# Decode attention: y accumulated as 4 rows of 128 columns and stored in 256-byte pieces

## The chip, the cores and the metric

The kernel runs on one core of a Trainium2 chip. The profile shows five engines that work side by side: TensorE (PE, busy for 479.8 us of the span of 680.7 us in the kernel before, with its weight loads as PEld, 264.9 us), VectorE (DVE, 377.8 us), ScalarE (ACT, 42.5 us), GpSimd (POOL, 2.4 us) and SyncE (SP), which here issues loads and stores. In the kernel they wait for one another by semaphores. The page counts 16 DMA engines; in the kernel before they read 285.21 MB from HBM, nearly all of it into a ring in the on-chip memory SBUF. The kernel has PE's sums in tensors of PSUM. The metric is the time of one execution on the device in microseconds (us). Each profile is one execution; its span is 1.7 to 2.0 us shorter than the reported time of the same run.

## The reference, cut to what matters

Two independent attention problems A and B of one query token, with the same shapes; the outputs are concatenated.

```python
# x (1,1,512)  k,v (1,32,8192,128)  wq (512,4096)  wo (4096,512), all bf16
q = (x @ wq) as 32 heads of 128
scores = einsum("bhqd,bhkd->bhqk", q, k) * 128 ** -0.5
o = softmax(scores) @ v                # 32 heads of 128 numbers
y = o.reshape(1, 1, 4096) @ wo         # 512 numbers for each problem
out = concatenate([y_A, y_B], axis=-1) # 1024 bf16, 2 KB
```

K and V of both problems are 268 MB, and each number is used once. The output is 2 KB.

## The kernel before

The heads are done in pairs: `j` runs over 32 pairs, 16 of A and 16 of B. Each K or V of a pair is one load of 4 MB into a ring of five slots; all loads are issued by SyncE. For a pair, DVE multiplies K by q, PE adds up partial columns with an identity matrix ("fold"), DVE, PE and ACT do the softmax, and PE multiplies V by the probabilities ("PV": 128 matmuls with a moving operand of 2 columns).

The part that the change touches is y = o times W_o. Each head needs four matmuls, each of which loads a 128x128 block of W_o as weights and streams one column of o. The 512 outputs lie in PSUM as 128 partitions of 4 columns, so that the store writes 128 pieces of 8 bytes:

```python
def plan_y(a, h0, n, pm):            # heads h0..h0+n of problem a
    ...
    wo = ring[...].rearrange("p (h m b) -> p h m b", h=H, b=NB)      # NB = 4
    for i in range(n):
        for b in range(NB):
            m = e.matmul(y_ps[:, b:b + 1], wo[:, h0 + i, :, b],
                         src[:, a, h0 + i:h0 + i + 1], ...)
    if lastblk:
        ...
        ve = INC('DVE', c_ye, lambda e: e.tensor_copy(y_sb[:, a, :], y_ps[:, 0:NB]))
        W('SP', c_ye, ve)            # the store waits in SyncE's program order
        ... e.dma_start(out[0, 0, a * NOUT:(a + 1) * NOUT].rearrange("(p b) -> p b", b=NB),
                        y_sb[:, a, :])                               # issued by SP
```

The y of A is computed some 400 us into the run, while loads of B stream. The y of B ends the run. Its heads come in groups: 16, 8 and 4 heads while the last pair's softmax is under way, then two heads after PV(30) and two after PV(31):

```python
j = NPR - 1                          # 31, the last pair
plan_R(j, 1); plan_w_ready(j - 2)
plan_y(LA, *ys.pop(0))               # 16 heads, 64 matmuls
plan_m1(j); plan_tr(j)               # maxima of the pair; transposed on PE
plan_y(LA, *ys.pop(0))               # 8 heads, 32 matmuls
plan_m2(j); plan_bc(j); plan_exp(j); plan_sum(j); plan_ri(j)
for b in ys: plan_y(LA, *b)          # 4 heads, 16 matmuls
for i in range(2):
    plan_PV(j - 1 + i); plan_o(j - 1 + i)
    plan_y(LA, *direct_l[i])         # 2 heads, 8 matmuls
```

## Time and profile before

| | before |
|---|---|
| time, median of 3 runs (lowest, highest) | 683.43 us (682.38, 684.32) |
| span of the profile | 680.7 us |
| last K landed / last V landed | 643.7 / 674.9 us |
| last store: issued / landed | 676.54 / 680.30 us |

Landing times that no line below shows are read from the landing records of the trace: the moments at which a transfer's semaphore is counted up.

From the page of the kernel before, the DMA rows of the 40 time slices: the busy share in tenths, then the rate.

```profile
span 680.7 us, 12357 instructions
...
DMA  9999999999999999999999999999999999999993
GB/s 370 431 430 431 431 433 429 429 430 430 427 435 433 428 430 432 430 426 430 431 430 429 431 430 430 428 405 432 429 432 432 428 426 430 430 430 433 422 415 131
```

The DMA engines are busy from end to end at about 430 GB/s, so the run is bound by loads; one slice, the 27th, shows 405. The next view gives three stretches of 12 us: length, then busy time of PE, PEld, DVE, ACT and POOL (with the number of instructions), granted PE clock (the share of its full speed that PE was allowed), DMA share and, last, GB/s.

```profile
423.00:435.00 12.00, 11.47 (x159) 6.84 (x160) 8.70 (x13) 0.04 (x1) 0.00 (x0) 0.86 1.00 426
...
439.00:451.00 12.00, 6.43 (x144) 4.63 (x141) 3.73 (x5) 0.00 (x0) 0.00 (x0) 0.84 1.00 392
451.00:463.00 12.00, 8.93 (x26) 3.56 (x27) 7.84 (x12) 1.14 (x5) 0.00 (x0) 0.64 1.01 437
```

In the middle stretch the DMA engines are as busy as ever but move 392 GB/s. In exactly this stretch the 128 small writes of A's y are carried out (their packets start between 439.55 and 447.23 us): they wait in the queue behind loads, and their landing records lie between 440.2 and 447.8 us, the last 37.4 us after the issue. The view of the tile `y_sb` gives both stores, A's and B's:

```profile
L552 SPq DMA_DIRECT2D out_dram<-y_sb x2: 344/388/431, 410.4 to 676.5; - x2
...
DMA to landing us min/median/max: 3.8/20.6/37.4
```

The tail is read from the chain of waits, the work that ended last, in order of time (start, length, what):

```profile
605.27 38.42 DMA ring<-in_B_k_cache_dram
...
648.41 5.31 PE fold L374 x16
...
656.47 3.63 PE fold L374 x16
...
660.18 2.14 PE yps L537 x64
...
662.52 1.03 PE yps L537 x32
...
665.93 0.52 PE yps L537 x16
666.46 3.43 PE otps L459 x128
...
670.13 0.43 PE yps L537 x8
...
670.88 1.51 issue
672.39 3.25 PE otps L459 x116
...
676.35 0.16 DVE y_sb L546
```

From the landing of the last K at 643.7 us on, PE, DVE and ACT work in turn: two folds, the y groups between the steps of the softmax, PV(30) from 666.46, PV(31) with a pause of 1.51 us after its first 12 matmuls, the cast, and then the store. "issue" marks time in which the engine waited for nothing that the profile shows.

### The profile page before, as it was taken

To read this page: it belongs to the slowest core of one execution; us is meant where nothing else is said; L and a number is where in the kernel's file an instruction comes from. 1 tells how busy PE (TensorE), PEld (TensorE's weight loads), DVE (VectorE), ACT (ScalarE), POOL (GpSimd) and SP (SyncE) were. 2 spreads that over 40 slices of the span, in tenths; PEclk is the share of its full clock that TensorE was granted. 3 is DMA by queue.
4 is the path that set the end of the run, shared out by engine and by line. 5 is a ranking of instruction groups with operands and counts; after the bars stand their busy time and mean duration, and the time that the engine had idled before them with its cause. 6 is when DMAs were issued, how large, how long until landed. Compare 5 with 4: busy or idle time off the path is not lost.

```text
span 680.7 us, 12357 instructions
## 1 busy us (share of the span) xinstructions
PE 479.8 (70%) x5660; PEld 264.9 (39%) x5660; DVE 377.8 (56%) x513; ACT 42.5 (6%) x169; POOL 2.4 (0%) x16
## 2 busy tenths in 40 slices
PE   0487877767688767856777576857768768667775
PEld 0133533434343434433433352534434234334445
DVE  4158556655555665555556526656555557463650
ACT  0110000000000000000000000000000001000000
POOL 1000000000000000000000000000000000000000
PEclk9998867877876867789867786967887668678885
DMA  9999999999999999999999999999999999999993
GB/s 370 431 430 431 431 433 429 429 430 430 427 435 433 428 430 432 430 426 430 431 430 429 431 430 430 428 405 432 429 432 432 428 426 430 430 430 433 422 415 131
DMA packets 11684, 286.01 MB, mean 420 GB/s; under 512 B 1776, under 2 KB 2288, under 8 KB 2672
## 3 DMA queue, kind: packets, MB, share of 16 engines
q1 hardware_dynamic: 11344, 285.22, 97.9%
q8 instruction: 44, 0.72, 0.4%
q14 instruction: 8, 0.07, 0.0%
q10 hardware_dynamic: 288, 0.00, 0.0%
HBM read 285.21 MB, written 0.00 MB: 419 GB/s over the span
## 4 chain that ended last, share of the span: by engine, by line
DMA 53%; PE 30%; DVE 12%; issue 3%; ACT 1%; ACTq 0%; DVEq 0%
DMA ring<-in_B_k_cache_dram 27%; DMA ring<-in_A_k_cache_dram 22%; PE fold L374 19%; DVE ring L361 11%; PE otps L459 7%; DMA xT<-in_B_x_dram 3%; PE qwps L333 2%; PE yps L537 1%; ACT qbc L340 1%; DVE m L410 1%; ACT p L429 0%; PE stps L436 0%; PE stps L405 0%; DVE wt L504 0%; PE stps L415 0%
## 5 line engine op out<-in xcount | busy, mean ns | idle before, releaser
L374 PE MATMUL fold<-ring,ident 128*128 128x512 bf16 x1024 | 320.5, 484 | 109.7 <-DVE ring L361 109.2
L361 DVE TENSOR_TENSOR ring<-ring,qbc 128x2048 bf16<-128x2048 bf16 x256 | 300.9, 1216 | 148.5 <-DMA ring<-in_A_k_cache_dram 84.9
L374 PEld LDWEIGHTS fold<-ring,ident 128*128 128x128 bf16 x1024 | 117.3, 120 | 287.8 <-issue 117.5
L459 PEld LDWEIGHTS otps<-p,ring 128*128 128x128 bf16 x4096 | 108.3, 97 | 8.7 <-issue 1.6
L459 PE MATMUL otps<-p,ring 128*128 128x2 bf16 x4096 | 108.3, 163 | 1.5 <-issue 1.5
L387 DVE TENSOR_REDUCE s_sb<-fold 128x64 f32<-128x512 f32 x64 | 43.1, 674 | 10.7 <-PE fold L374 10.3
L410 DVE TENSOR_REDUCE m<-stps 2x1 f32<-2x128 f32 x32 | 8.9, 279 | 69.8 <-PE stps L405 69.8
L436 PE MATMUL stps<-rowsum,ones_f 128*128 128x2 f32 x64 | 13.6, 282 | 41.5 <-ACT p L429 41.5
L421 ACT COPY nb<-stps 128x1 f32<-128x1 f32 x32 | 5.1, 159 | 580.3 <-PE stps L415 580.3
L333 PE MATMUL qwps<-ring,xsel 128*128 128x512 bf16 x64 | 16.7, 408 | 29.2 <-DVE xsel L226 24.3
L429 ACT ACTIVATE p<-s_sb,nb 64x128 bf16<-64x128 f32 x64 | 27.9, 436 | 2.1 <-ACT nb L421 0.3
L436 PEld LDWEIGHTS stps<-rowsum,ones_f 128*128 128x128 f32 x64 | 10.8, 211 | 44.2 <-ACT p L429 44.2
L333 PEld LDWEIGHTS qwps<-ring,xsel 128*128 128x128 bf16 x64 | 6.0, 103 | 39.4 <-issue 27.2
L415 PE MATMUL stps<-m,sel 2*128 2x1 f32 x64 | 12.3, 259 | 11.5 <-DVE m L410 11.5
L415 PEld LDWEIGHTS stps<-m,sel 2*128 2x128 f32 x64 | 9.6, 186 | 24.0 <-DVE m L410 24.0
L397 DVE TENSOR_REDUCE m<-s_sb 64x1 f32<-64x128 f32 x64 | 17.7, 277 | 1.0
L504 DVE TENSOR_TENSOR wt<-qwps,hmask 128x512 f32<-128x512 f32 (+3 forms) x5 | 2.2, 440 | 24.6 <-PE qwps L497 24.5
L429 ACT ACTIVATION_READ_ACCUMULATOR p<-s_sb,nb 64x1 f32 x64 | 11.7, 182 | 0.0
L475 DVE TENSOR_TENSOR ot<-otps,rinv 128x2 bf16<-128x2 f32 x32 | 4.9, 154 | 11.8 <-PE otps L459 11.8
L537 PE MATMUL yps<-w_bf,ring 128*128 128x1 bf16 x240 | 8.7, 172 | 1.9 <-issue 1.9
L537 PEld LDWEIGHTS yps<-w_bf,ring 128*128 128x128 bf16 x240 | 8.6, 118 | 1.9 <-issue 1.9
L405 PE MATMUL stps<-ident_f,m 128*2 128x128 f32 x32 | 8.8, 275 | 0.0
(30 smaller groups left out, 34.4 us busy)
## 6 DMA issues: line engine op xcount, KB each, us to landing
ring<-in_A_k_cache_dram SPq DMA_DIRECT2D x16, 4096.0 KB, 37.1
ring<-in_A_v_cache_dram SPq DMA_DIRECT2D x16, 4096.0 KB, 31.0
ring<-in_B_k_cache_dram SPq DMA_DIRECT2D x16, 4096.0 KB, 37.8
ring<-in_B_v_cache_dram SPq DMA_DIRECT2D x15, 4096.0 KB, 31.9
ring<-in_A_wq_dram SPq DMA_DIRECT2D x1, 4096.0 KB, 12.5
ring<-in_B_wq_dram SPq DMA_DIRECT2D x1, 4096.0 KB, 21.9
ring<-in_A_wo_dram SPq DMA_DIRECT2D x1, 4096.0 KB, 36.5
ring<-in_B_wo_dram SPq DMA_DIRECT2D x1, 2048.0 KB, 20.2
```

Of the source, the lines that this page charges most:

```text
L333: m = e.matmul(qw_ps[:, :].rearrange("p (j d) -> p j d", d=Dh), xsel[:, a, c, par, :], wq[:, c, 4 * g:4 * g + 4, par, :], start=(i == 0), ...
L361: m_val[(j, i)] = INC('DVE', c_m, lambda e: e.tensor_tensor(t, t, qbc[:, a, jj:jj + 1, :].broadcast_to([P, CH, Dh]), ALU.mult))
L374: m = e.matmul(fold_ps[h][:, :].rearrange("p (t e) -> p t e", e=FE), ident[:], t[:, h * HT:(h + 1) * HT, c * FE:(c + 1) * FE], start=(c == ...
L387: r_val[(j, h)] = INC('DVE', c_r, lambda e: e.tensor_reduce(s_sb[:, j % 2, h * HT:(h + 1) * HT], fold_ps[h][:, :].rearrange("p (t e) -> p ...
L397: m1_val[j] = INC('DVE', c_m1, lambda e, h=h, q0=q0, q1=q1: e.tensor_reduce(m1[q0:q1, j % 2, h:h + 1], s_sb[q0:q1, j % 2, :], AX.X, ALU.max))
L405: tr_val[j] = INC('PE', c_tr, lambda e: e.transpose(st_ps[j % 2][0:2, 0:P], m1[:, j % 2, :], ident_f[:]))
L410: m2_val[j] = INC('DVE', c_m2, lambda e: e.tensor_reduce(m2[0:2, j % 2:j % 2 + 1], st_ps[j % 2][0:2, 0:P], AX.X, ALU.max))
L415: bc_val[j] = INC('PE', c_bc, lambda e: e.matmul(st_ps[j % 2][:, P:P + 1], sel2[:], m2[0:2, j % 2:j % 2 + 1], start=True, stop=True))
L429: e_val[j] = INC('ACT', c_e, lambda e, h=h, q0=q0, q1=q1: e.activation(p2[q0:q1, j % 2, :, h], s_sb[q0:q1, j % 2, :], AF.Exp, bias=nb[q0:q ...
L436: s_val[j] = INC('PE', c_s, lambda e: e.matmul(st_ps[j % 2][:, P + 2:P + 4], ones_f[:], rowsum[:, j % 2, :], start=True, stop=True))
L459: m = e.matmul(ot_ps[j % 2][:, 0:2], t[:, i, :], p2[:, j % 2, i, :], start=(i == 0), stop=(i == TP - 1))
L537: m = e.matmul(y_ps[:, b:b + 1], wo[:, h0 + i, :, b], src[:, a, h0 + i:h0 + i + 1], start=(first and i == 0 and b == 0), stop=(lastblk and ...
```

## The change

The intent: write the output in longer pieces. The roles in the y matmul are swapped. W_o streams, 128 columns at a time, and the weights are a narrow matrix of 4 columns, one of which holds o. For each head, `sq` is a 4x4 square with o on its diagonal, so that matmul `b` uses row `b` of the square and adds its 128 numbers to row `b` of PSUM. y is then 4 partitions of 128 columns, and a store is four pieces of 256 bytes. The y of A is stored from ACT's queue instead of SyncE's.

```diff
-        y_sb = ec(nc.sbuf_tensor("y_sb", [P, NA, NB], BF16))
+        y_sb = ec(nc.sbuf_tensor("y_sb", [NB, NA, P], BF16))
+        sq = ec(nc.sbuf_tensor("sq", [P, NA, H, NB * NB], BF16))
...
     # plan_o, last two pairs: o straight onto the diagonal
+                o_val[j] = INC('DVE', c_o, lambda e: e.tensor_tensor(
+                    sq[:, a, 2 * jj:2 * jj + 2, 0:NB * NB:NB + 1], ...))
...
     # plan_w, other heads: one more DVE copy onto the diagonal
+                w_val[(a, h0)] = INC('DVE', c_w, lambda e, i0=i0: e.tensor_copy(
+                    sq[:, a, h0 + i0:h0 + i0 + ni, 0:NB * NB:NB + 1], ...))
...
-                    "p (h m b) -> p h m b", h=H, b=NB)
+                    "p (h b m) -> p h b m", h=H, b=NB)
...
-                        m = e.matmul(y_ps[:, b:b + 1], wo[:, h0 + i, :, b], src[:, a, h0 + i:h0 + i + 1],
+                        m = e.matmul(y_ps[0:NB, 0:P], sq[:, a, h0 + i, b * NB:(b + 1) * NB],
+                                     wo[:, h0 + i, b, :],
...
-                W('SP', c_ye, ve)
+                q = 'SP' if a == LA else 'ACT'
+                W(q, c_ye, ve)
...
-                            out[0, 0, a * NOUT:(a + 1) * NOUT].rearrange("(p b) -> p b", b=NB),
+                    out[0, 0, a * NOUT:(a + 1) * NOUT].rearrange("(b m) -> b m", b=NB),
```

## The prediction

> **What bounds the kernel.** DMA. In the span of 680.7 us the page's DMA row reads 9 nearly everywhere, at about 430 GB/s; SyncE's waits for free slots (484.5 us on the PE fold) hide behind queued loads. The tail differs: the last K lands at 643.7 us, then (chain of waits, timeline) fold to 660.1, y matmuls of early heads (64, 32, 16) between softmax steps, PV(30) 666.3 to 669.9, 8 y matmuls, PV(31) to 675.6 with a 1.51 us stall at 670.9, 8 y matmuls, cast at 676.35, store issued at 676.54, landed 3.8 us later. The last V piece lands at 674.9 in the landing records: DMA and PE end nearly together.
>
> **What the change removes.**
> 1. The first y store (128 pieces of 8 B) sits in the SP queue among the loads and lands 37.4 us after issue. Windows show 392 GB/s over 439 to 451 us, 429 to 431 around it: about 0.09 of 12 us, so 1 us of every DMA engine, critical. [...] Worth 0.6 to 1.0 us.
> 2. The last store: its landing records spread over 678.0 to 680.3 us, as 16 engines finish 8 small writes each. With 4 pieces I expect 1.6 to 2.2 us from issue to landing, not 3.8. Worth 1.6 to 2.2 us, all critical.
>
> **What it adds.**
> 1. Each y matmul loads 4 columns and streams 128; before, 128 loaded and 1 streamed. Before: 64 in 2.28 us, 36 ns each. After: the fold takes 227 ns per 512 columns at full clock and 427 at half (timeline), so I estimate 57 to 65 ns each warm and 107 cold. [...] The granted clock is 0.50 after 665 us, so the late ones are cold. On the tail chain the 64 delay the transpose of the maxima by about 1.4 us, the 32 the broadcast by 0.6, the 16 add 0.3 to 1.1, and the two groups of 8 add 0.2 to 0.5 each: 2.5 to 4 us, partly returned because the 1.51 us stall, [...], should shrink when PE comes later.
> 2. First problem: 128 y matmuls at 403 to 410 us take 7 to 14 us instead of 6.4. Off the path: several loads of 9.7 us each are queued.
> 3. The cast reads 128 elements per partition, not 4: about 0.28 us (the maximum over 2x128 takes 0.279), not 0.16. Diagonal copies and memset are hidden.
>
> **Sum.** −0.8 (first store) −1.9 (last store) +1.9 (y in the tail, net of the stall's return, 0.5 to 3.5) +0.1 = about −1 us: 682.4 us, range 680.2 to 684.6. Faster by over 2%: 0.01; within 2%: 0.98; slower: 0.01.
>
> **What would show it.** GB/s near 440 to 460 us level at about 430; last V landing about 1 us earlier; last store landing under 2.3 us after issue; y matmuls at 57 to 65 ns in the first group, about 107 in the last; PV(30) starting 1 to 3 us later; a shorter stall.
>
> **What would make it wrong.** Load-plus-stream pairs well over 65 ns warm; HBM writes landing no sooner in 256 B pieces; the stall not shrinking; the first store's cost not being on the slowest engine's path.

The sum came to −0.8 − 1.9 + 1.9 + 0.1 = −0.7 us, put as about −1 us. The first term rests on the dip to 392 GB/s alone. The pace of 57 and 107 ns stands as an estimate from the fold's 227 and 427 ns for 512 columns, a quarter of each.

## The result, and the profile after

| | before | after |
|---|---|---|
| first comparison: median (lowest, highest) | 683.3 us (682.38, 684.32), 4 runs | 684.04 us (683.82, 684.24), 4 runs |
| ratio of after to before, 95% interval | | 1.001 (0.9993 to 1.0028) |
| second comparison (after_2 below): median | 682.87 us, 11 runs | 682.38 us (681.78, 684.26), 6 runs |
| ratio, 95% interval | | 0.9996 (0.9979 to 1.0012) |

A ratio is the mean time of one kernel's runs over that of the other's of the same rounds, so it is not quite the ratio of the medians. The kernel was neither faster nor slower. What matters is where the gains went.

The first store. The same view of stretches, after:

```profile
439.00:451.00 12.00, 9.19 (x148) 5.83 (x148) 6.98 (x9) 1.14 (x5) 0.00 (x0) 0.86 1.02 437
451.00:463.00 12.00, 9.48 (x37) 4.14 (x38) 7.30 (x12) 1.14 (x5) 0.00 (x0) 0.86 1.00 430
```

The dip is gone. The last K lands at 642.76 us instead of 643.69, the last V at 674.00 instead of 674.88.

The last store. SyncE's wait at the end of the program for the output to land (total, times, longest), first before, then after:

```profile
SPq L99 <- DMA out_dram<-y_sb: 3.4, 1, 3.4
```

```profile
SPq L100 <- DMA out_dram<-y_sb: 0.8, 1, 0.8
```

From the issue at 680.17 us to the last landing record at 681.36 us it took 1.19 us. Before, it took 3.8.

The tail, from the chain of waits of the changed kernel:

```profile
606.79 35.97 DMA ring<-in_B_k_cache_dram
...
647.47 6.26 PE fold L378 x16
...
656.48 5.18 PE fold L378 x16
...
661.74 3.67 PE yps L550 x64
...
665.60 1.88 PE yps L550 x32
...
669.46 0.98 PE yps L550 x16
670.44 3.33 PE otps L463 x128
...
674.03 1.01 PE yps L550 x8
675.04 3.52 PE otps L463 x128
...
678.82 1.03 PE yps L550 x8
...
679.87 0.28 DVE y_sb L561
```

Three things differ. The y groups take 3.67, 1.88 and 0.98 us instead of 2.14, 1.03 and 0.52, and the last two 1.0 us each instead of 0.43. The pause inside PV(31) is gone. And the two folds, which the change does not touch, take 6.26 and 5.18 us instead of 5.31 and 3.63.

The second profile of the unaltered changed kernel, after_2, shows that the folds are a matter of the run, not of the kernel:

```profile
647.41 5.09 PE fold L378 x16
...
655.25 3.63 PE fold L378 x16
...
667.66 3.31 PE otps L463 x128
...
672.65 0.63 issue
673.28 3.25 PE otps L463 x116
```

With folds alike, the two kernels can be compared stage by stage. Each row is a difference of times in the chain of waits; the last two use the landing records and the span.

| stage | before | after_2 | difference | after, first profile: difference from before |
|---|---|---|---|---|
| start to last K landed | 643.69 | 642.70 | −0.99 | −0.93 |
| to the end of the last fold | 16.41 | 16.18 | −0.23 | +2.49 |
| to the start of PV(30) | 6.36 | 8.78 | +2.42 | +2.42 |
| to the end of PV(31) | 9.18 | 8.86 | −0.32 | −1.06 |
| to the end of the cast | 0.87 | 1.59 | +0.72 | +0.72 |
| to the landing of the last store | 3.79 | 1.21 | −2.58 | −2.58 |
| to the end of the span | 0.40 | 0.73 | +0.33 | +0.34 |
| sum | 680.70 | 680.05 | −0.65 | +1.40 |

The two stores won 0.99 + 2.58 = 3.57 us. The tail gave back 2.42 − 0.32 + 0.72 = 2.82 us, for y matmuls that are slower and a larger cast, and 0.1 us elsewhere. What is left is 0.65 us, which the 2 us that one run of this kernel differs from the next hides.

### The profile page after: what moved, and what is told of

It reads as the page before. It is cut to its first block, busy times and chain, and to the rows that moved or that the text cites. A ratio compares the mean times of both kernels' runs of the same rounds, so it can differ in the third digit from the quotient of the medians.

```text
span 682.1 us, 12363 instructions
## 1 busy us (share of the span) xinstructions
PE 481.2 (71%) x5660; PEld 270.6 (40%) x5660; DVE 379.1 (56%) x519; ACT 42.5 (6%) x169; POOL 2.5 (0%) x16
## 2 busy tenths in 40 slices
DMA packets 11411, 286.00 MB, mean 419 GB/s; under 512 B 1504, under 2 KB 2016, under 8 KB 2400
## 4 chain that ended last, share of the span: by engine, by line
DMA 53%; PE 32%; DVE 12%; issue 2%; ACT 1%; ACTq 0%; DVEq 0%
DMA ring<-in_B_k_cache_dram 27%; DMA ring<-in_A_k_cache_dram 22%; PE fold L378 19%; DVE ring L365 11%; PE otps L463 7%; DMA xT<-in_B_x_dram 3%; PE yps L550 3%; PE qwps L337 2%; ACT qbc L344 1%; DVE m L414 1%; PE stps L409 0%; DVE wt L514 0%; DVE w_bf L523 0%; ACT p L433 0%; DVE xsel L230 0%
## 5 line engine op out<-in xcount | busy, mean ns | idle before, releaser
L378 PE MATMUL fold<-ring,ident 128*128 128x512 bf16 x1024 | 312.9, 475 | 115.0 <-DVE ring L365 114.9
L378 PEld LDWEIGHTS fold<-ring,ident 128*128 128x128 bf16 x1024 | 115.4, 118 | 287.6 <-DVE ring L365 120.4
L550 PE MATMUL yps<-ring,sq 128*4 128x128 bf16 x256 | 18.9, 244 | 0.5 <-DVE sq L480 0.5
L550 PEld LDWEIGHTS yps<-ring,sq 128*4 128x4 bf16 x256 | 17.5, 96 | 0.9 <-DVE sq L480 0.7
```

Of the source, the lines that this page charges most:

```text
L378: m = e.matmul(fold_ps[h][:, :].rearrange("p (t e) -> p t e", e=FE), ident[:], t[:, h * HT:(h + 1) * HT, c * FE:(c + 1) * FE], start=(c == ...
L550: m = e.matmul(y_ps[0:NB, 0:P], sq[:, a, h0 + i, b * NB:(b + 1) * NB], wo[:, h0 + i, b, :], start=(first and i == 0 and b == 0), stop=(las ...
```

## The experiments

Twelve kernels ran, in three sets; each set has its own runs of the kernel before. "Ratio" is always to those. All gave the reference's output except the two marked.

| run | median us | before, same set | ratio (95% interval) |
|---|---|---|---|
| t_first | 682.15 | 682.75 | 0.999 (0.9976 to 1.0004) |
| t_last | 681.24 | 682.75 | 0.9973 (0.9959 to 0.9987) |
| t_both | 681.02 | 682.75 | 0.9971 (0.9957 to 0.9985) |
| after_order | 682.42 | 682.75 | 0.9985 (0.997 to 1.0) |
| first_act8 | 683.66 | 683.88 | 1.0003 (0.9978 to 1.0027) |
| first_sp256 | 683.84 | 683.88 | 1.0002 (0.998 to 1.0024) |
| last8 (wrong) | 685.64 | 683.88 | 1.0029 (1.0005 to 1.0052) |
| shift64 | 683.09 | 683.88 | 1.0003 (0.9971 to 1.0035) |
| after_2 | 682.38 | 682.87 | 0.9996 (0.9979 to 1.0012) |
| after_warm | 680.42 | 682.87 | 0.9962 (0.9948 to 0.9976) |
| t_order | 680.05 | 682.87 | 0.9958 (0.9944 to 0.9972) |
| last32 (wrong) | 682.27 | 682.87 | 0.9994 (0.9976 to 1.0012) |

None differs from the kernel before by 2%; the interval leaves out 1 for t_last, t_both, after_warm and t_order (shorter) and for last8 (longer).

### The two stores without the new matmuls: t_first, t_last, t_both

These keep the one-column y matmuls and turn the finished y on PE, one small transpose for a problem, for A only, for B only, and for both.

```diff
+ y_f = ec(nc.sbuf_tensor("y_f", [P, NA, NB], F32))
+ y_t = ec(nc.sbuf_tensor("y_t", [NB, NA, P], BF16))
-    "p (h m b) -> p h m b", h=H, b=NB)
+    "p (h b m) -> p h b m" if a in TR else "p (h m b) -> p h m b", h=H, b=NB)
+ if a in TR:                                   # TR = (0,), (1,) or (0, 1)
+     tensor_copy(y_f[:, a, :], y_ps[:, 0:NB])                       # DVE
+     transpose(y_ps[0:NB, P:2 * P], y_f[:, a, :], ident_f[:])       # PE
+     tensor_copy(y_t[:, a, :], y_ps[0:NB, P:2 * P])                 # DVE
+     store y_t[:, a, :] as "(b m) -> b m", from ACT for A, from SP for B
```

> The kernel before; only y of the first problem is transposed on TensorE (after a copy to SBUF) and stored in four 256-byte pieces from the ACT queue; y matmuls keep one moving column; the last store stays 128 pieces of 8 bytes. Theory (the first store's 8-byte pieces cost every DMA engine about 0.9 us and the run is DMA bound): no dip to 392 GB/s in 439 to 451 us, last K and last V land 0.8 to 1.0 us earlier than in the kernel before (643.7 and 674.9), the time is 0.5 to 1.0 us shorter, last store still about 3.8 us from issue to landing. Rival (the tail hides what the loads win): V lands earlier, but the time stays within 0.3 us of before.

Measured: the window 439 to 451 us shows 433 GB/s, no dip. The last V landed at 674.20 us. The mean time is 682.23 us against 682.87, 0.6 us less, but the interval of the ratio includes 1. So the loads do end earlier; that the time follows is likely and not shown by this run alone.

> The kernel before; only y of the second problem is transposed on TensorE and stored in four 256-byte pieces; its W_o weights are read contiguously. Theory: last store lands 1.2 us after issue instead of 3.8 (as after the change), the added copy, transpose and copy cost about 0.8 us, so the time is 1.5 to 2.2 us shorter; the last V still lands at about 674.9. Rival (the short landing in the changed kernel comes from the DMA queues being idle longer before it, not from the pieces): landing stays near 3 us and the time is within 0.5 us or longer.

Measured: issued to landed about 1.2 us, the last V at 674.86 us, and 1.8 us less in the mean (681.04 against 682.87), as the theory had it. The rival, that the DMA queues had only been idle for longer, is settled by last8 below: its small pieces were issued 5.3 us after the last V had landed, later than the 3.7 us here, and still took 3.6 us. So the gain of the last store is in the pieces.

> Both of the above. Theory (the two gains add): 2.3 to 3.0 us shorter than before, about 680.7 us, and the same below the changed kernel 684.0 by 3 us or more, since the stores are the same and only the y matmul form differs. Rival (the form of the y matmuls costs nothing in the tail and the changed kernel is slow for the clock phase alone): within 1 us of the changed kernel.

Measured: 2.1 us less than before in the mean (680.73 against 682.87), a little under what was expected; the first store adds only 0.3 us to t_last, within the scatter. Against the changed kernel the ratio is 0.9971 / 0.9996 (after_2, another set) = 0.9975, about 1.7 us less, where 3 us was expected from the unlucky first measurement of 684.04. The timeline of t_both shows what binds its tail, with PE now early enough:

```profile
672.67 0.58 PE L463 MATMUL otps<-p,ring 128*128 128x2 bf16 x16 [0.23 <-DMA ring<-in_B_v_cache_dram]
...
673.91 0.58 PE L463 MATMUL otps<-p,ring 128*128 128x2 bf16 x16 [0.66 <-DMA ring<-in_B_v_cache_dram]
...
675.38 0.38 PE L553 MATMUL yps<-ident_f,y_f 128*4 128x128 f32 x1 [0.26 <-DVE y_f L551]
...
675.79 0.28 DVE L556 CAST y_t<-yps 4x128 bf16<-4x128 f32 x1 [0.47 <-PE yps L553]
```

PV(31) waits for each part of the last V: the tail is bound by the loads, as it should be. The transpose with its copies adds about 0.74 us: from the end of the last y matmul to the end of the cast it takes 0.93 us here (675.14 to 676.07), and 0.19 in the kernel before (676.32 to 676.51).

### Piece size or queue: first_act8, first_sp256

The change altered both for A's store. Each run undoes one of them.

```diff
 first_act8, from the kernel before
-                W('SP', c_ye, ve)
+                q = 'SP' if a == NA - 1 else 'ACT'
+                W(q, c_ye, ve)             # and the store is issued from q
 first_sp256, from the changed kernel
-                q = 'SP' if a == LA else 'ACT'
+                q = 'SP'
```

> The kernel before with the first y store issued from the ACT queue, still 128 pieces of 8 bytes. Theory (the piece size costs, not the queue): the DMA engines still lose 0.7 to 1.0 us each, now soon after 410 us (the dip moves there), the store lands within some 10 us of issue, and last K and V land as before. Rival (the place in the SP queue costs): no dip, last K and V 0.9 us earlier.

> The changed kernel with the first y store back on the SP queue, still four 256-byte pieces. Theory: no dip anywhere, the store lands some 30 to 37 us after issue, last V lands as in the changed kernel (674.0 in its profile) and the time is within 0.4 us of the changed kernel. Rival: the dip of 0.9 us is back and the time 0.9 us longer.

Windows of first_act8:

```profile
411.00:423.00 12.00, 8.56 (x25) 3.50 (x26) 8.52 (x13) 1.14 (x5) 0.00 (x0) 0.64 1.00 410
...
439.00:451.00 12.00, 9.27 (x150) 5.92 (x148) 6.55 (x8) 1.14 (x5) 0.00 (x0) 0.86 1.00 431
```

Windows of first_sp256:

```profile
439.00:451.00 12.00, 9.25 (x148) 5.84 (x148) 6.82 (x8) 1.14 (x5) 0.00 (x0) 0.86 1.01 434
```

With 8-byte pieces on ACT's queue the dip moved to the stretch after 411 us; it landed 15.3 us after issue, later than the 10 us expected, and the last V landed at 674.78 us, as before. With 256-byte pieces on SyncE's queue there is no dip, though the store again waited among the loads (issued at 411.8, landed at 443.2 us), and the last V landed at 674.13. The piece size costs, and the queue does not. How deep the dip is varies: in 439 to 451 us the three profiles with an 8-byte first store from SyncE show 392 (before), 403 (shift64) and 414 GB/s (t_last), the ten with 256-byte pieces 425 to 437. Over all profiles: the last V landed at 674.88, 674.86, 674.78 and 674.22 us with an 8-byte first store (mean 674.69) and between 673.68 and 674.20 us in the ten with 256-byte pieces (mean 673.93), 0.76 us earlier. The 674.22 of shift64 lies outside its group, and why is open.

### What a store of small pieces costs: last8, last32

From the changed kernel, the last store is cut into pieces of 8 or 32 bytes that are interleaved by partition. The second half of the output is therefore permuted.

```diff
-    out[0, 0, a * NOUT:(a + 1) * NOUT].rearrange("(b m) -> b m", b=NB), y_sb[:, a, :]
+    dst.rearrange("(g b e) -> b g e", b=NB, e=4),        # last32: e=16
+    y_sb[:, a, :].rearrange("b (g e) -> b g e", e=4)     # last store only
```

> The changed kernel with the last store cut on purpose into 128 pieces of 8 bytes from its 4 partitions, to places interleaved by partition, so the second half of the output is permuted (a wrong result on purpose). Theory (each small HBM write takes its time on its engine, 8 per engine took 1.5 to 3.8 us from issue): 32 pieces on each of 4 engines land 5 to 10 us after issue and the time grows by 4 to 9 us. Rival (the number of engines or partitions sets the landing): 1.2 us as in the changed kernel.

> As last8 (landing 3.6 us after issue with 128 pieces of 8 bytes on 4 engines), but 32 pieces of 32 bytes, again permuted on purpose. Theory (a store to HBM takes a time for each piece, whatever engine it comes from: 2.4 us more for 124 more pieces): about 1.7 to 1.9 us from issue to landing. Rival (pieces below some size are slow however few): 3 us or more. Second rival (pieces do not matter at 32 bytes): 1.2 us.

Measured: last8 was issued at 679.36 us and landed at 682.99, 3.6 us. That is as long as in the four profiles that store the same 128 pieces from 128 partitions (3.8 us before, 3.5 to 3.6 in t_first, first_act8 and shift64), although 4 engines here did the pieces that 16 engines did there. (The engines are inferred from the traces: beside its pieces the last store has 4 packets of 4 bytes in the changed kernel, 16 in the kernel before, and 4 again in last8, where the page counts 1,628 packets under 512 bytes against 1,504 in the changed kernel, 124 more; the landing records below agree.) The theory that each engine pays for each of its pieces expected 5 to 10 us, and falls; so does its rival, which expected 1.2. last32 was issued at 680.10 us and landed at 681.37, 1.27 us: 32 pieces of 32 bytes cost no more than four of 256. The expected 1.7 to 1.9 us of a cost that grows in step with the number of pieces falls too. Whether 8 bytes are too short or 128 too many is not separated by these runs. What holds is that 128 pieces of 8 bytes cost about 2.4 us more than 4 or 32 longer ones, whether 4 or 16 engines write them. The DMA packet records of the packed traces add where the time passes. In last8 the 128 packets start between 680.15 and 680.58 us and the landing records of their 4 engines lie between 682.56 and 682.99; in the kernel before they start between 677.38 and 677.56 and land between 678.03 and 680.30. The four 256-byte packets of the changed kernel start by 681.00 and have landed by 681.36. So most of the time passes after the packets have started, which goes with the number of engines not mattering; what takes it is open.

### Where the y matmuls stand in the tail: after_order

The same instructions of the changed kernel, with the groups in another order, so that more of them fall into times when PE waits for DVE or ACT.

```diff
-        plan_y(LA, *ys.pop(0))      # 64 matmuls
+        plan_y(LA, *y8)             # 32
         plan_m1(j); plan_tr(j)
-        plan_y(LA, *ys.pop(0))      # 32
+        plan_y(LA, *y4)             # 16
         plan_m2(j); plan_bc(j)
+        plan_y(LA, *y16)            # 64
         plan_exp(j); plan_sum(j); plan_ri(j)
-        for b in ys: plan_y(LA, *b) # 16
```

> The changed kernel with the last groups of y matmuls in another order in the tail: 32 before the transpose of the maxima, 16 before the broadcast, 64 while ScalarE takes the exponentials. Same instructions. Theory (128-column y matmuls delay the softmax chain of the last head pair): about 1.6 us shorter than the changed kernel, PV(30) starts about 7.2 us after the last fold ends instead of 8.8. Rival (y is not on the chain): within 0.4 us of the changed kernel.

Measured: from the end of the last fold (662.15 us) to the start of PV(30) (669.59 us) it took 7.44 us instead of 8.78, close to the 7.2 expected. So the y matmuls do stand on the chain. The time, 682.42 us, is 1.6 us under the 684.04 that it was to be compared with, but that is not like for like: the unaltered kernel later measured 682.38. The ratios, 0.9985 and 0.9996, differ by 0.7 us within their intervals.

### The pause inside PV(31): shift64

From the kernel before, with 64 idle matmul pairs (a weight load and a matmul each) at the start, while PE waits for x.

```diff
+        def shift(e):
+            for i in range(64):
+                e.matmul(st_ps[0][:, 0:2], ident[:], ones_b[:, 0:2], start=True, stop=True)
+        OP('PE', shift)
         for a in range(NA):
             for g in range(GQ):
                 plan_q(a, g)
```

> The kernel before with 64 idle matmul pairs (128 PE instructions) at the start, while PE waits for x, [...]. Theory (the 1.51 us pause of PE at the 12th matmul of PV(31) and the 1.85 us pause in the first y group are waits for an instruction fetch): both pauses leave their places; pauses, if any, are 64 pairs off (84th of PV(30) or 76th of PV(31)). Rival (the pause of PV(31) is the wait for V's second part, which lands at the same moment): it stays where it was, and ends when that part lands.

Timeline of shift64 (the last group of numbers in brackets is idle time before it, and what ended it):

```profile
669.77 1.84 PE L459 MATMUL otps<-p,ring 128*128 128x2 bf16 x64
...
671.77 0.51 PE L459 MATMUL otps<-p,ring 128*128 128x2 bf16 x13 [0.15 <-DMA ring<-in_B_v_cache_dram]
...
673.53 1.52 PE L459 MATMUL otps<-p,ring 128*128 128x2 bf16 x51 [1.25 <-issue]
```

The pause, 1.25 us here, comes after 64 + 13 = 77 matmuls of PV(31), where it had come after 12. In the first y group it moved from after 33 matmuls to after 98. Both moved by 65 where 64 was expected; a record more or less can be lost. The rival, the wait for V's second part, falls: that wait is there too, named, and at its own place, after the 64th. So the pause belongs to a place in PE's instruction stream, and the packet records show instruction transfers of 16,384 bytes that go with it: 44 in the kernel before, with 11,450 recorded PE instructions (260 for each), and 45 in shift64, with 11,577 (257 for each). One of them ends at 670.91 us in the kernel before and at 672.06 in shift64; in both PE goes on about 1.5 us later (672.39 and 673.53). That the pause is a wait for such a transfer is inferred from this, and why it takes that long after the transfer is open. With a transfer for every 257 to 260 instructions on average, about 129 pairs, a place that comes 64 pairs earlier is followed by the next one 65 pairs after the old place, which agrees with the 65. The pause does not need full DMA engines: their busy share was 0.45 from 669.90 to 672.40 us, around the pause of the kernel before in PV(31), and 0.93 from 404.40 to 406.73, around the one in the first y group.

### The granted clock: after_2, after_warm

after_2 is the changed kernel unaltered. after_warm adds idle matmuls of 512 columns where PE waits before the two last folds.

```diff
+            if j == NPR - 1:
+                warm(9)             # before the first fold of the last K
...
                 plan_bc(j - 1)
+                if j == NPR - 1:
+                    warm(4)         # before the exponentials of pair 30
# warm(n): n matmuls into qw_ps, ident as weights, selw[16] streamed, 512 columns
```

> The changed kernel again, unaltered, beside the next three on the same chip. Every theory: 683.5 to 684.5 us, spread under 1 us. It gives a second profile of the tail: if the slow folds of the last K (6.26 and 5.18 us for 16 matmuls, against 5.31 and 3.63 in the kernel before) are the phase of the granted clock and not the change, they may come out otherwise here, by 1 to 2.5 us, with the time of that run moving along; if the change causes them they come out the same.

> The changed kernel with 9 idle matmuls of 512 columns on TensorE before the first fold of the last K, while PE waits for it, and 4 before the exponentials of head pair 30, so that the clock is granted before the folds. Theory (the tail of the changed kernel is bound by PE at half clock): the two folds come nearer to 3.63 us each, PV(30) starts 2 to 4 us earlier than 670.4, and the time is 2 to 3.5 us shorter, 680.5 to 682 us; beyond that the last V (674.0) binds. Rival (the tail is bound by the loads in the changed kernel too): no gain, or longer by up to 1 us.

The stretches of the two last folds: the third number from the right is the granted PE clock. The changed kernel, first profile:

```profile
648.00:652.00 4.00, 4.00 (x11) 1.38 (x10) 2.91 (x5) 0.00 (x0) 0.00 (x0) 0.50 1.05 426
...
656.00:660.00 4.00, 3.78 (x12) 1.47 (x13) 1.09 (x3) 0.00 (x0) 0.00 (x0) 0.57 0.95 406
```

after_2:

```profile
648.00:652.00 4.00, 4.00 (x15) 1.56 (x13) 2.85 (x5) 0.00 (x0) 0.00 (x0) 0.70 1.05 426
...
656.00:660.00 4.00, 4.00 (x38) 2.45 (x37) 1.02 (x4) 0.00 (x0) 0.00 (x0) 1.00 0.99 422
```

after_warm:

```profile
648.00:652.00 4.00, 3.63 (x18) 1.55 (x16) 3.67 (x7) 0.00 (x0) 0.00 (x0) 1.00 1.01 410
...
656.00:660.00 4.00, 4.00 (x53) 3.04 (x52) 1.58 (x6) 0.00 (x0) 0.00 (x0) 1.00 1.00 426
```

The folds took 6.26 and 5.18 us at clocks of 0.50 and 0.57, 5.09 and 3.63 at 0.70 and 1.00, and about 3.6 each at 1.00 in after_warm. In these traces the granted clock changes only at multiples of 3.41 us from an offset of its own: 0.89 us from the start of the span in the first profile of the changed kernel, 1.87 us in after_2, 0.06 us in the profile before. In the two profiles of the changed kernel the last K landed at 642.76 and 642.70 us, so the loads do not explain the difference. That the same program gets its folds at full or at half clock by the luck of that offset is inferred from this. after_2 measured 681.78, 681.94, 681.82, 683.82, 684.26 and 682.82 us; the profile is of the first of these, and the first profile of the changed kernel is of a run of 683.82. The spans of the two profiles differ by 2.05 us. The first four runs of the changed kernel, 683.82 to 684.24, all lie at the slow end.

after_warm took away the luck: six runs between 680.15 and 680.9 us, mean 680.45, 2.3 us under after_2's 682.74 of the same set, as expected. Its PV(30) starts at 666.59 us. The tail of the changed kernel was bound by PE. The 13 idle pairs also move the pause inside PV(31) from after its 12th matmul to just before PV(31), where it is 0.45 us long and not 0.63 as in after_2; that is little of the 2.3.

Slow folds are not a mark of the 128-column y: t_last, with one-column y, had 6.57 and 5.31 us. Of the six profiles with 128-column y without warming, five had a last fold of over 5 us; of the seven with one-column y, three. Whether the change shifts the odds is open; these are too few.

### The best order and the best store together: t_order

t_both with the order of after_order.

> Both stores transposed (as t_both), with the other order of the last y groups. Theory (with one-column y matmuls the tail waits for the last V, which its chain of waits shows): no gain over t_both, 680.4 to 681.2 us, PV(31) again ends by the last V part, and some 3 us below the changed kernel. Rival (PE still binds): 0.7 us or more below t_both.

Measured: 680.05 us, ratio 0.9958 to before. Its profile, of the slowest of its six runs, fell on slow folds (6.45 and 5.29 us) and still started PV(30) at 666.84 us, since the y groups now lie where PE would wait. Against t_both's 0.9971 the gain is 0.9 us with intervals that overlap, so neither theory is settled by the times. In the profile the theory missed: PV(31) ended at 675.65 us after a pause like that of shift64, of 1.24 us and after its 11th matmul, and not by the last V, which landed at 673.90. Both t_order and after_warm beat the kernel before and the changed kernel, by about 0.4% each. Beside after_2 of the same set, t_order is 0.9958 / 0.9996 = 0.9962.

## Why the prediction was right

It said 682.4 us, 680.2 to 684.6, and the same within 2% with 0.98. The first measurement was 684.04, the second 682.38. That alone proves little: the range is wider than the scatter of the kernel before (682.38 to 684.32), and the gain of 1 us in the sum is not shown by the times, as the medians differ by +0.7 and by −0.5 us with intervals that include a ratio of 1. Point by point, against the comparison with like folds (before and after_2):

- **First store, −0.8 us, with 0.6 to 1.0.** The dip is gone, the last K lands 0.93 to 0.99 us earlier, and the last V 0.76 us earlier over all profiles. Right, with the mechanism that first_act8 and first_sp256 separate: piece size. The landing records of the changed kernel's last store, from 4 rows, are one 0.5 us after the issue and four later (681.30 to 681.36 us), where the 128-row store of the kernel before has sixteen (678.03 to 680.30 us).
- **Last store, −1.9 us.** Right in kind and too small: 2.58 us, since it landed after 1.2 us and not after 1.6 to 2.2. The reason given, that 16 engines finish 8 small writes each, does not explain the time: in last8 4 engines with 32 each took as long.
- **Pace of y, 57 to 65 ns warm (granted clock 1.00) and 107 ns cold (0.50).** Right: 3.67 us / 64 = 57 ns, and the starts of the last 8 matmuls lie 100 ns apart. The two groups of 8 take 1.01 and 1.03 us with their drain at the half clock; after_order had the group of 8 before PV(31) at full clock, 0.61 us. That every late group would be cold was wrong: the clock stayed at 1.00 in 664 to 672 us (to 670.88 us in after_2), where it had been 0.50, so only the groups of 8 paid. That the wider y matmuls kept it up is inferred.
- **Tail, +1.9 us net of the pause's return, and +0.1 for the cast.** With like folds it was +2.42 − 0.32 + 0.72 = +2.82 us, 0.8 us more than the sum: in after_2 the pause shrank to 0.63 us and not to zero. In the first profile, where it vanished, the same three rows make +2.08.
- **First problem's y off the path.** It took 10.10 us, between 7 and 14, and K and V landed no later.
- **PV(30) 1 to 3 us later.** 1.2 us in after_2, 4.0 us in the first profile. Here the prediction missed a term: it left the folds of the last K at the length that the one profile before happened to show. The offset of the clock moved them by 2.5 us, more than the net effect that was predicted. That the first median lies 1.6 us above the prediction goes with the slow folds of its profile.

The mis-sized terms, the last store (0.7 us too small) and the tail (0.8 us too small), nearly cancelled: the sum of −0.65 us in the table is close to the −1 us of the prediction partly for that reason.

## What to carry to other kernels

Write a small output in few pieces (here four landed 2.6 us sooner after the issue than 128), but do not choose the form of the matmuls for the sake of the store: one transpose of the finished result cost about 0.7 us, and streaming W_o instead of o cost 2.4 us on the last chain before PV(30). Look at what stands on the chain after the last load, and put other work of that engine where it would wait anyway. Before explaining a difference of a few microseconds, compare instructions that the change did not touch; here identical folds differed by 2.5 us with the granted clock, and a few idle matmuls before them were worth more than the change.

## What the traces show of the hardware

- PE paused in PV(31) and in the first y group, where the profile shows nothing that it waited for: 1.25 and 2.33 us in shift64, 1.51 and 1.85 us in the kernel before. It went on 1.2 us (first y group, kernel before) and 1.5 us (PV(31), both) after the end of an instruction transfer of 16,384 bytes.
- With weights of 4 columns, a pair of weight load and 128-column matmul took 57 ns (3.67 us / 64, changed kernel) at a granted clock of 1.00.
- With W_o's columns 4 elements apart a one-column pair took 33 ns (2.14 us / 64, kernel before); with adjacent columns it took 25 ns (1.60 us / 64, t_last, where 95 pairs of the A group, with the step, took 3.29 us, 35 ns each).
- In the kernel before, PE was busy, by the modelled ends of its matmuls, for the whole of the 3.41 us from 665.67 to 669.08 us (one- and two-column matmuls), and the clock stayed at 0.50 from 662.25 us to the end of the run.
- From issue to landing of the last store, 128 pieces of 8 bytes took 3.5 to 3.8 us, 32 of 32 bytes 1.27, 4 of 256 bytes 1.17 to 1.19; and in the profiles with 128 pieces of 8 bytes among the loads the last V landed about 0.8 us later.
